# Attention and soft mixture of experts: products on a tile of ones before the first loads, the first turned pairs in another PSUM ring, a new order of the first pair, and its negated row maxima on ScalarE

## The chip, the cores and the metric

The kernel runs on one core of a Trainium2 chip. The time is the device time of one execution in microseconds (us). Beside plain runs there is one profiled execution, whose trace gives each instruction of each engine: TensorE (PE for the products, PEld for the loads of weights), VectorE (DVE), ScalarE (ACT), GpSimd (POOL) and SyncE (SP).

## The reference

The input is `q`, `k` and `v` for 8 batches, 12 heads, 448 positions and 64 features a head, and a soft mixture of experts with 32 slots, 8 experts, a model width of 768 and a hidden width of 1024. In short:

```
scores = scale * q @ k.T                       # per batch and head, 448 x 448
m      = max(scores, -1);  e = exp(scores - m)
x      = (e / (sum(e) + exp(-m) + 1e-9)) @ v   # heads side by side: 3584 x 768
logits = x @ phi                               # 3584 x 32
slot_in  = softmax(logits over the rows).T @ x # 32 x 768
slot_out = relu(slot_in @ w1[e]) @ w2[e]       # four slots for each expert
out      = softmax(logits over the slots) @ slot_out
```

## The kernel before, in words

Two heads make a **pair**; there are 48 pairs (`NPAIR`), six to a batch, and three pairs (`NP`) make a group `g` of loads. The order of all instructions is written out by hand (`manual_schedule`, L59), and each engine takes its own instructions in the order of the program. Loads are issued from POOL's queue (`gdma`, L57), the results at the end from SP's.

The work on pair `n` has these parts:

- `T(n)` (L214) turns q and k with 28 small transposes on PE (L224) into one PSUM bank `ps_t`; ACT copies the bank to SBUF for `n < 6` (L227, a "T copy" below).
- `A(n, i)` (L237), four a pair, multiplies query rows by all keys (L246, L256) into banks `ps_a`, and DVE takes the row maximum of each (L250, L259). For `i < 3` there are two banks and two maxima (one for each head `hl`), for `i = 3` one bank and one maximum; a pair has 7 maxima. `A1(n, i, hl)` (L261) does one head of an `A` alone.
- `W1(g)` (L273) writes the negated maxima on POOL: three instructions into the rows `wm` (the function `neg`, L277), then `ngm`, a rounded copy. `W2(g)` (L293) turns `wm` on PE into a bank `ps_m`, and `W3(g)` (L301) copies that on ACT to `mT` (L303) and takes two small exponentials (L306, L309).
- `Bk(n, i)` (L313) makes the scores with the keys as rows in banks `ps_b`: the product (L332), then a product that subtracts the maxima from `mT` (L335), then ACT's exponential (L338). From half-step 5 on, `AB` (L342) does the same with an `A1` around it (L354, L358, L360, maxima L268, L270).
- `AV(n, i, ...)` (L381) multiplies by v into the one bank `ps_av`; `N1`, `N2` (L399, L408) divide; `PX` (L438) turns the result, and `P(b)` (L458) does the softmax of the slots for a batch.

PSUM has three rings in this part: `psA` with three banks (tag "a": `ps_a`, `ps_t` and the banks of `P`), `psB` with four (tag "b": `ps_b`, `ps_m`, `ps_x`) and `psV` with one. A tile takes the next bank of its ring and waits until the last reader of that bank is done.

The main loop (L635) goes over the pairs `s`, each in two half-steps `hs = 2s + y`. In the half-steps 0 to 4 each does four `A` of later pairs (`As(1)`, four times), two `Bk` of pair `s`, one `T(hs + 3)` and, from half-step 1 on, an `AV`. Ahead of the loop stands a prologue (L610 to L625): `T(0)`, `A` 0 and 1 of pair 0, `T(1)`, `A` 2 and 3, `W1(0)`, the copy `V(0)` of v on POOL, a load of v, `A(1, 0)`, `T(2)`, `W2(0)`, `W3(0)`, `A(1, 1)`, then loads of group 2 and four rewrites of weights (`narrow`, L136). The first half-step starts with `A(1, 2)`. The loads of group 0 (one for each pair), of v and of group 1 are the first instructions of the program (L170 to L177), with `make_identity` between them; DVE's fills (L190 to L201) stand behind.

Of the kernel before, what the change touches and what calls it, by code (L numbers as in the profile page):

```python
# [8 lines left out]
F32 = mybir.dt.float32  # L9
BF16 = mybir.dt.bfloat16  # L10
AX = mybir.AxisListType
AF = mybir.ActivationFunctionType
ALU = mybir.AluOpType
# [11 lines left out]
HG = 6  # L25
NP = 3
W65 = 65
# [4 lines left out]
def kernel(  # L32
# [10 lines left out]
    nc = tc.nc  # L43
    B, H, S, D = q.shape
# [27 lines left out]
    ones = const.tile([128, 2], BF16, name="ones")  # L72
    sel = const.tile([128, HG], BF16, name="sel")
    phi_sb = const.tile([128, KC, NS], BF16, name="phi_sb")
    halfm = const.tile([128, 2], F32, name="halfm")
# [13 lines left out]
    part = lambda nm, o, z: R[:, at_[nm] + o:at_[nm] + o + z]  # L89
# [3 lines left out]
    vp = [part(f"vp{i}", 0, VPN).rearrange("p (h i d) -> p h i d", h=HG, i=4) for i in range(2)]  # L93
    wm = [part(f"wm{i}", 0, 512).rearrange("p (i c) -> p i c", i=4) for i in range(2)]
# [48 lines left out]
    with ExitStack() as at:  # L143
# [3 lines left out]
        psA = pool("psA", 3, space=PSUM)  # L147
        psB = pool("psB", 4, space=PSUM)
# [5 lines left out]
        def load(g, nm, l0=0, l1=NP):  # L154
# [12 lines left out]
                gdma(out=t[64:128], in_=x[:, :, 3:7, :])  # L167
            nat[nm, g] = t

        for pl in range(NP):  # L170
            load(0, "q", pl, pl + 1)
            load(0, "k", pl, pl + 1)
            if pl == 0:
                make_identity(nc, ident)
# [9 lines left out]
        for base in (0, 64):  # L184
# [2 lines left out]
                out=sel[base:base + 64], in_=sel[base:base + 64], fill=1.0,  # L187
                compare_op=ALU.not_equal, base=0,
                pattern=[[-1, HG]], channel_multiplier=1)
        nc.vector.memset(halfm, 0.0)  # L190
        for hl in range(2):
            nc.vector.memset(halfm[64 - 64 * hl:128 - 64 * hl, hl:hl + 1], 1.0)
        for t in wm:
            nc.vector.memset(t, 0.0)
        for t in vp:
            nc.vector.memset(t, 0.0)
            nc.vector.memset(t[:, :, 0:3, D:W65], 1.0)
            nc.vector.memset(t[0:64, 0:HG:2, 3, D:W65], 1.0)
            nc.vector.memset(t[64:128, 1:HG:2, 3, D:W65], 1.0)
        nc.vector.memset(ones, 1.0)  # L200
        nc.vector.memset(ones[64:128, 1:2], 0.0)  # L201
        gdma(out=phi_sb, in_=moe_phi.rearrange("(j p) s -> p j s", p=128))

        mx, ngm, ec, mT, eT, av, us = {}, {}, {}, {}, {}, {}, {}
# [8 lines left out]

        def T(n):  # L214
            g, pl = divmod(n, NP)
            ps = psA.tile([128, 2, S], BF16, tag="a", name="ps_t")
            for a in range(2):
                src = nat["qk"[a], g]
                for tok in range(7):
                    for hl in range(2):  # L220

                        c = kcol(hl, tok) if a else (2 * tok if tok < 4 else 2 * tok - 7) * 64
                        r = slice(64 * hl, 64 * hl + 64)
                        nc.tensor.transpose(ps[r, a, c:c + 64], src[r, pl, tok * D:(tok + 1) * D], ident[r, r])  # L224
            t = qk_t[n % NQK]
            if n < 6 or pl == 0:
                nc.scalar.copy(t, ps)  # L227
            else:
                nc.vector.tensor_copy(t, ps)  # L229
            qkT[n] = t  # L230
# [30 lines left out]
        def A1(n, i, hl):  # L261

            g, pl = mg(n), n % NP
            if pl == mpl(g)[0] and i == 0 and hl == 0:
                mx[g] = psm.tile([128, 21], F32, tag="mx", name="mx")
            t, r = qkT[n], slice(64 * hl, 64 * hl + 64)
            ps = psA.tile([128, 512], F32, tag="a", name="ps_a")
            nc.tensor.matmul(ps[:, 0:S], t[r, 0, i * 128:(i + 1) * 128], t[r, 1, :], start=True, stop=True)  # L268
            c = HG * i + 2 * pl + hl
            nc.vector.reduce_max(mx[g][:, c:c + 1], ps[:, 0:S], axis=AX.X)  # L270


        def W1(g):  # L273
            w, m = wm[g % 2], mx[g]
            l0, l1 = mpl(g)
            nm = psm.tile([128, 21], BF16, tag="ngm", name="ngm")
            neg = lambda o, s: nc.gpsimd.tensor_scalar(o, s, -1.0, None, op0=ALU.mult)  # L277
            cols = lambda t: t[:, 0:3 * HG].rearrange("p (i c) -> p i c", i=3)[:, :, 2 * l0:2 * l1]
            o = w[:, 0:3, :].rearrange("p i (d c) -> p i d c", d=2)[:, :, :, 2 * l0:2 * l1]
            neg(o, cols(m).unsqueeze(2).to_broadcast([128, 3, 2, 2 * (l1 - l0)]))  # L280
            for hl in range(2):
                r = slice(64 - 64 * hl, 128 - 64 * hl)
                o = w[r, 3, :].rearrange("p (d c) -> p d c", d=2)[:, :, 2 * l0 + hl:2 * l1:2]
                neg(o, m[r, 3 * HG + l0:3 * HG + l1].unsqueeze(1).to_broadcast([64, 2, l1 - l0]))
            if l1 - l0 == NP:
                neg(nm, m)
            else:
                nc.gpsimd.memset(nm, 0.0)
                neg(cols(nm), cols(m))
                neg(nm[:, 3 * HG + l0:3 * HG + l1], m[:, 3 * HG + l0:3 * HG + l1])  # L290
            ngm[g] = nm
# [313 lines left out]
        def As(c):  # L605
            for _ in range(min(c, len(runs))):
                A(*runs.pop(0))


        T(0)  # L610
        As(2)
        T(1)
        As(2)
        W1(0)
        V(0)
        load(1, "v")
        As(1)
        T(2)
        W2(0)
        W3(0)  # L620
        As(1)
        for nm in "qk":
            load(2, nm)
        for z in range(4):
# [10 lines left out]
        for s in range(NPAIR):  # L635
# [57 lines left out]
            g = (s + 10) // 3  # L693
# [193 lines left out]
```

## Time and profile before

| what | value |
|---|---|
| median of 3 runs | 310.43 us (310.2 to 311.73) |
| profiled execution | 310.7 us |
| its span, first to last instruction | 308.9 us |
| busy in the span | PE 275.6, DVE 257.2, ACT 249.3, POOL 202.7 us |
| chain of waits that ended last | PE 50%, DVE 30%, ACT 7% |

A line of the timeline has the start, the length, the engine, the source line (L224 is line 224), the operation, what it writes and reads, how many instructions are merged in it, and in brackets how long the engine had idled and what ended that. A line of the page's groups has the busy time, the mean of one instruction in ns and the idle time before.

### The profile page before, as it was taken

What the parts mean: (1) busy time and instruction counts of PE and PEld (TensorE: products, weight loads), DVE (VectorE), ACT (ScalarE), POOL (GpSimd) and SP (SyncE); (2) the same over time, 40 slices, a digit from 0 to 9 for tenths busy, and PEclk for the clock granted to TensorE, in tenths of its full rate; (3) what the DMA queues carried; (4) which work ended last, traced back from release to release, by engine and by line L of the source; (5) the groups of instructions that cost most, each with busy time, mean ns of one, the idle gap of its engine ahead of it and who ended that gap; (6) DMA issues with size and microseconds to landing.
All of it is one profiled execution on the core that took longest, in us unless ns stands there. A gap on an engine that the chain in (4) does not pass through costs nothing.

```text
span 308.9 us, 12205 instructions
## 1 busy us (share of the span) xinstructions
PE 275.6 (89%) x5067; PEld 159.0 (51%) x5068; DVE 257.2 (83%) x607; ACT 249.3 (81%) x549; POOL 202.7 (66%) x403
## 2 busy tenths in 40 slices
PE   2899999999999999999999999999999899994810
PEld 1434456565666656665566566656665556451200
DVE  4778999999999999999999999999999566536930
ACT  2357599999999999999999999999999997236810
POOL 8682769788788878896889788879584863000000
PEclk9999999999999999999999999999999999999555
DMA  6999499999999999999999999999971999937997
GB/s 88 149 128 202 64 205 150 198 182 205 163 196 157 210 169 198 155 203 149 149 164 186 177 186 169 196 177 203 166 110 17 144 126 204 337 128 260 415 439 312
DMA packets 49350, 57.44 MB, mean 186 GB/s; under 512 B 2832, under 2 KB 41488, under 8 KB 48912
## 3 DMA queue, kind: packets, MB, share of 16 engines
q0 software_dynamic: 45536, 42.52, 90.1%
q1 hardware_dynamic: 3760, 14.16, 11.5%
q8 instruction: 39, 0.64, 0.8%
q14 instruction: 15, 0.12, 0.1%
HBM read 88.18 MB, written 14.16 MB: 331 GB/s over the span
## 4 chain that ended last, share of the span: by engine, by line
PE 50%; DVE 30%; ACT 7%; issue 4%; POOL 4%; DMA 1%; DVEq 0%; POOLq 0%
DVE mx L270 15%; PE ps_av L393 11%; PE ps_a L268 6%; PE ps_t L224 6%; PE ps_b L354 5%; PE ps_b L358 4%; DVE mx L250 3%; DVE mx L259 3%; PE ps_b L332 3%; PE ps_a L246 2%; DVE W L801 2%; DVE R L229 2%; PE ps_x L445 2%; ACT R L227 2%; PE ps_so L764 2%
## 5 line engine op out<-in xcount | busy, mean ns | idle before, releaser
L270 DVE TENSOR_REDUCE mx<-ps_a 128x1 f32<-128x448 f32 x248 | 136.6, 613 | 5.3 <-PE ps_a L268 5.1
L360 ACT ACTIVATE R<-ps_b 128x448 bf16<-128x448 f32 x272 | 131.0, 573 | 1.1 <-PE ps_b L358 0.8
L268 PE MATMUL ps_a<-R 64*128 64x448 bf16 x248 | 80.5, 352 | 1.8 <-DVE mx L270 1.8
L354 PE MATMUL ps_b<-R 64*128 64x448 bf16 x272 | 73.9, 353 | 0.9
L358 PE MATMUL ps_b<-mT,sel 64*128 64x448 bf16 x272 | 70.6, 350 | 0.0
L393 PEld LDWEIGHTS <-R 128*128 128x128 bf16 (+1 forms) x1536 | 50.5, 101 | 30.5 <-issue 26.4
L393 PE MATMUL ps_av<-R 128*128 128x65 bf16 (+1 forms) x1536 | 64.9, 196 | 0.1
L419 POOL TENSOR_TENSOR R<-ubuf,rec 128x384 bf16<-128x384 f32 x44 | 36.3, 825 | 37.9 <-DVE rec L415 23.4
L224 PEld LDWEIGHTS <-R 64*64 64x64 bf16 x1344 | 31.1, 113 | 19.2 <-issue 7.8
L338 ACT ACTIVATE R<-ps_b 128x448 bf16<-128x448 f32 x64 | 36.0, 579 | 5.9 <-PE ps_b L335 5.9
L224 PE MATMUL ps_t<-ident,R 64*64 64x64 bf16 x1344 | 32.0, 198 | 5.9 <-DMA R<-in_q_dram 4.3
L451 ACT CAST R<-ps_x 128x512 bf16<-128x512 f32 x47 | 28.1, 598 | 5.7 <-PE ps_x L445 5.7
L259 DVE TENSOR_REDUCE mx<-ps_a 128x1 f32<-128x448 f32 x48 | 29.6, 616 | 0.6 <-PE ps_a L256 0.3
L358 PEld LDWEIGHTS <-sel 64*128 64x128 bf16 x272 | 21.5, 94 | 14.9 <-issue 5.3
L268 PEld LDWEIGHTS <-R 64*128 64x128 bf16 x248 | 23.1, 94 | 9.8
L405 ACT COPY ubuf<-ps_av 128x455 f32<-128x455 f32 x44 | 25.2, 573 | 3.0 <-PE ps_av L393 2.8
L227 ACT COPY R<-ps_t 128x896 bf16<-128x896 bf16 x20 | 18.4, 922 | 11.3 <-PE ps_t L224 11.0
L250 DVE TENSOR_REDUCE mx<-ps_a 128x1 f32<-128x448 f32 x40 | 22.6, 618 | 4.3 <-PE ps_a L246 3.9
L332 PE MATMUL ps_b<-R 64*64 64x448 bf16 (+1 forms) x112 | 22.7, 386 | 0.0
L335 PE MATMUL ps_b<-mT,sel 64*64 64x448 bf16 (+1 forms) x112 | 21.5, 366 | 0.0
L424 POOL TENSOR_TENSOR R<-ubuf,rec 128x128 bf16<-128x128 f32 x44 | 17.5, 398 | 3.7
L354 PEld LDWEIGHTS <-R 64*128 64x128 bf16 x272 | 17.2, 94 | 4.7 <-issue 0.2
(132 smaller groups left out, 454.0 us busy)
## 6 DMA issues: line engine op xcount, KB each, us to landing
W<-in_moe_w_dram POOLq DMA_DIRECT2D x22, 768.0 KB, 9.5
R<-in_v_dram POOLq DMA_DIRECT2D x32, 192.0 KB, 4.6
out_dram<-W SPq DMA_DIRECT2D x2, 2688.0 KB, 10.3
R<-in_q_dram POOLq DMA_DIRECT2D x15, 336.0 KB, 7.4
R<-in_k_dram POOLq DMA_DIRECT2D x15, 336.0 KB, 8.5
wd<-in_moe_w_dram POOLq DMA_DIRECT2D x8, 384.0 KB, 10.0
R<-wd SPq DMA_DIRECT2D x8, 384.0 KB, 8.6
R<-in_moe_w_dram POOLq DMA_DIRECT2D x2, 768.0 KB, 8.3
```

What stands on the lines that cost most here:

```text
L224: nc.tensor.transpose(ps[r, a, c:c + 64], src[r, pl, tok * D:(tok + 1) * D], ident[r, r])
L250: nc.vector.reduce_max(mx[g][:, c:c + 1], pss[hl][:, 0:S], axis=AX.X)
L259: nc.vector.reduce_max(mx[g][:, c:c + 1], ps[:, 0:S], axis=AX.X)
L268: nc.tensor.matmul(ps[:, 0:S], t[r, 0, i * 128:(i + 1) * 128], t[r, 1, :], start=True, stop=True)
L270: nc.vector.reduce_max(mx[g][:, c:c + 1], ps[:, 0:S], axis=AX.X)
L332: nc.tensor.matmul(outs[hl], t[rs[hl], 1, cols], t[rs[hl], 0, :], start=True, stop=False)
L338: nc.scalar.activation(e, p[:, 0:S], AF.Exp, scale=scale)
L354: nc.tensor.matmul(ps[hl][:, 0:S], t[rs[hl], 1, cols], t[rs[hl], 0, :], start=True, stop=False)
L358: nc.tensor.matmul(ps[hl][:, 0:S], sel[rs[hl], h:h + 1].to_broadcast([64, 128]), mT[mg(n)][rs[hl], :], start=False, stop=True)
L360: nc.scalar.activation(e[:, hl, :], ps[hl][:, 0:S], AF.Exp, scale=scale)
L393: nc.tensor.matmul(o, eT[n, i, hl][:, qc], vp[g % 2][:, 2 * pl + hl, i, 0:W65], start=(i == 0 and u == 0 and hl == 0), stop=(i == 3), skip ...
L419: eng.tensor_mul(x[:, 0:3, c:c + 128].rearrange("p i (h d) -> p i h d", h=2), u[:, 0:6, 0:D].rearrange("p (i h) d -> p i h d", h=2), rec[: ...
```

## The change

Six edits, all of them in the first microseconds:

1. A tile of 512 columns, `warm_t`, is filled with ones by DVE ahead of all else. `warm(n, cols)` multiplies it by itself `n` times into a bank of `psV` that nobody reads: seven products of 512 columns before the first transposes, two of 448 behind `T(0)`, one of 448 ahead of `A(0, 3)`.
2. DVE's fills move ahead of the first loads in the program; `ident2`, `identf` and `sel` come behind.
3. `T(n)` for `n < 6` takes its bank from `psB`, not `psA`.
4. The prologue is in another order: `A(0, 1)` is split, with `T(1)` between its heads; `T(2)` stands ahead of `W1(0)`; `A(1, 1)` is split, with `W2(0)` and `W3(0)` between its heads.
5. `W1(0)` writes its three instructions into `wm` on ACT (`rows`); `ngm` stays on POOL, and so do all later `W1`.
6. A helper `As1` does the halves.

```diff
+        warm_t = part("e2", 0, 512)
+        nc.vector.memset(warm_t, 1.0)
+        ps_w = psV.tile([128, 512], F32, tag="v", name="ps_warm")
+
+        def warm(n, cols=512):
+            for _ in range(n):
+                nc.tensor.matmul(ps_w[:, 0:cols], warm_t[:, 0:128], warm_t[:, 0:cols], start=True, stop=True)
...
+        warm(7)
+        for pl in range(NP):
+            load(0, "q", pl, pl + 1)
...
-            ps = psA.tile([128, 2, S], BF16, tag="a", name="ps_t")
+            tp, tg = (psB, "b") if n < 6 else (psA, "a")
+            ps = tp.tile([128, 2, S], BF16, tag=tg, name="ps_t")
...
+            rows = (lambda o, s: nc.scalar.mul(o, s, -1.0)) if g == 0 else \
+                (lambda o, s: nc.gpsimd.tensor_scalar(o, s, -1.0, None, op0=ALU.mult))
...
-            neg(o, cols(m).unsqueeze(2).to_broadcast([128, 3, 2, 2 * (l1 - l0)]))
+            rows(o, cols(m).unsqueeze(2).to_broadcast([128, 3, 2, 2 * (l1 - l0)]))
...
-                neg(o, m[r, 3 * HG + l0:3 * HG + l1].unsqueeze(1).to_broadcast([64, 2, l1 - l0]))
+                rows(o, m[r, 3 * HG + l0:3 * HG + l1].unsqueeze(1).to_broadcast([64, 2, l1 - l0]))
...
+        def As1(hl):
+            A1(*runs[0], hl)
+            if hl:
+                runs.pop(0)
+
         T(0)
-        As(2)
+        warm(2, S)
+        As(1)
+        As1(0)
         T(1)
-        As(2)
+        As1(1)
+        As(1)
+        warm(1, S)
+        As(1)
+        T(2)
         W1(0)
         V(0)
         load(1, "v")
         As(1)
-        T(2)
+        As1(0)
         W2(0)
         W3(0)
-        As(1)
+        As1(1)
```

More of the change, by code (lines that the diff above doesn't have):

```diff
@@ L168, in load @@
             nat[nm, g] = t
+        warm_t = part("e2", 0, 512)
[4 more added lines that the diff above has]
+                nc.tensor.matmul(ps_w[:, 0:cols], warm_t[:, 0:128], warm_t[:, 0:cols], start=True, stop=True)
+        nc.vector.memset(halfm, 0.0)
+        for hl in range(2):
+            nc.vector.memset(halfm[64 - 64 * hl:128 - 64 * hl, hl:hl + 1], 1.0)
+        for t in wm:
+            nc.vector.memset(t, 0.0)
+        for t in vp:
+            nc.vector.memset(t, 0.0)
+            nc.vector.memset(t[:, :, 0:3, D:W65], 1.0)
+            nc.vector.memset(t[0:64, 0:HG:2, 3, D:W65], 1.0)
+            nc.vector.memset(t[64:128, 1:HG:2, 3, D:W65], 1.0)
+        nc.vector.memset(ones, 1.0)
+        nc.vector.memset(ones[64:128, 1:2], 0.0)
+        warm(7)
         for pl in range(NP):
@@ L189 @@
                 pattern=[[-1, HG]], channel_multiplier=1)
[L190 to L201, printed above, removed]
         gdma(out=phi_sb, in_=moe_phi.rearrange("(j p) s -> p j s", p=128))
```

## Prediction

> **What bounds the kernel now.** I read the page first, then the waits, then the timeline of the first 30 us, then the groups of VectorE in that stretch. On the page:
>
> ```profile
> DVE  4778999999999999999999999999999566536930
> ...
> PEclk9999999999999999999999999999999999999555
> DMA  6999499999999999999999999999971999937997
> ...
> PE 50%; DVE 30%; ACT 7%; issue 4%; POOL 4%; DMA 1%; DVEq 0%; POOLq 0%
> ```
>
> From the fourth slice to the thirtieth DVE has nines, and yet the chain that ended last has more of PE than of DVE: the two release each other in turn, a machine in balance, in which a delay at the start is carried to the end. The first three slices (23 us) are thinner (4, 7, 7). The change touches only them. Of the answer on waits one line bears on loads:
>
> ```profile
> PE ps_t L224 <- DMA R<-in_q_dram: 4.3, 1, 4.3
> ```
>
> PE waits for a load once, for the first q; no later wait of PE, DVE or ACT for a load stands in that answer. The early timeline, cut to what the sum needs:
>
> ```profile
> 4.35 1.11 PE L224 MATMUL ps_t<-ident,R 64*64 64x64 bf16 x28 [4.35 <-DMA R<-in_q_dram]
> 5.50 0.91 ACT L227 COPY R<-ps_t 128x896 bf16<-128x896 bf16 x1 [3.47 <-PE ps_t L224]
> 7.06 2.22 DVE L250 TENSOR_REDUCE mx<-ps_a 128x1 f32<-128x448 f32 x4
> 16.08 0.56 PE L332 MATMUL ps_b<-R 64*128 64x448 bf16 x2
> 16.42 0.58 PE L335 MATMUL ps_b<-mT,sel 64*128 64x448 bf16 x2
> 19.47 0.56 PE L246 MATMUL ps_a<-R 64*128 64x448 bf16 x2 [0.32 <-DVE mx L250]
> 22.08 0.96 PE L224 MATMUL ps_t<-ident,R 64*64 64x64 bf16 x28
> 22.97 0.82 PE L393 MATMUL ps_av<-R 128*128 128x65 bf16 x12
> 24.12 2.22 DVE L250 TENSOR_REDUCE mx<-ps_a 128x1 f32<-128x448 f32 x4 [0.71 <-PE ps_a L246]
> 25.76 0.36 PE L332 MATMUL ps_b<-R 64*128 64x448 bf16 x2
> 25.96 0.35 PE L335 MATMUL ps_b<-mT,sel 64*128 64x448 bf16 x2
> 26.93 0.63 PE L224 MATMUL ps_t<-ident,R 64*64 64x64 bf16 x28 [0.18 <-DVE mx L259]
> 28.60 1.69 DVE L250 TENSOR_REDUCE mx<-ps_a 128x1 f32<-128x448 f32 x3 [0.67 <-PE ps_a L246]
> ```
>
> Two things are to be seen. First, **PE runs at half its rate until about 23 us**: L335 starts 0.34 us behind L332 at 16.1, and 0.20 behind it at 25.8; 28 transposes take 0.96 us at 22.08 and 0.63 at 26.93. PEclk has nines from the first slice, so that row doesn't show it; the products' spacing does. Second, DVE's gaps end on a product of `A` (0.71 and 0.67 us, <-PE ps_a). And a transposing `T` at full rate still waits for DVE (0.18 <-DVE mx L259), because `ps_t` takes its turn in the ring of the maxima's banks. How much DVE idles up to the 31st maximum, at 28.60, is in one row of the windows for DVE and in two of the groups:
>
> ```profile
> 7.00:28.58 21.58, 17.00 (x31) 1.00 1.14 155
> ```
> ```profile
> L250 DVE TENSOR_REDUCE mx<-ps_a 128x1 f32<-128x448 f32 x26 | 14.7, 618 | 3.4 <-PE ps_a L246 3.3
> L259 DVE TENSOR_REDUCE mx<-ps_a 128x1 f32<-128x448 f32 x4 | 2.5, 622 | 0.6 <-PE ps_a L256 0.3
> ```
>
> 30 maxima took 17.0 us, 0.567 each back to back, in 21.58: **4.58 us idle**. That is all there is to win without making a maximum shorter.
>
> The Trainium skill, "TensorE: Matmul & The Clock Gate", Part 1, has a rule for the first point: the array starts at half rate, and a free-running window of about 3.4 us with PE busy opens it. The trace agrees in that the last idle time of PE before the turn ends at 19.5 us and the full rate comes some 4 us later.
>
> **The change part by part.** *The seven products ahead of the loads.* The trace has no fill of 512 columns of ones and no such product at half rate. Bounds from these rows:
>
> ```profile
> 1.25 0.71 POOL L162 DMA_DIRECT2D R<-in_q_dram  x1 [0.79 <-POOLq L871]
> 1.95 0.55 POOL L162 DMA_DIRECT2D R<-in_k_dram  x1
> 3.59 0.54 POOL L162 DMA_DIRECT2D R<-in_k_dram  x1
> 3.85 0.55 DVE L194 MEMSET R<- 128x256 uint32 x2
> 4.51 0.72 DVE L196 MEMSET R<- 128x792 uint32 x1
> ```
> ```profile
> R<-in_k_dram POOLq DMA_DIRECT2D x1, 112.0 KB, 2.9
> ```
>
> 256 elements cost 0.27 (0.55 for two), 792 cost 0.72, so 512 about 0.48. POOL's first issue comes at 1.25, behind 0.79 of idle time, so from 0.46 on an engine may start; the ones are there at 0.95 to 1.75. A product of 448 columns follows the one before by 0.34 at half rate, so one of 512 by 0.39 (an estimate), and seven by 2.7. They end at 3.7 to 4.5. `T(0)` starts at 4.35 now; its second half needs the first k, issued at 1.95 and landed 2.9 later, at 4.85, so it ends near 5.4 in any case, and at 5.8 if a late last product and its drain hold it up by 0.3. At full rate the first pair's products come 0.1 to 0.2 earlier (0.20 against 0.34). Bounds at the start: 0.2 gained to 0.3 lost; I take 0, nearest to the 4.35 row. The two products behind `T(0)` (0.7) lie under the T copy (0.91); the one ahead of `A(0, 3)` lies in a wait for a bank.
>
> *DVE's fills* (0.48 + 0.55 + 2 x 0.72 and small ones, about 3 us) lie beside the first loads, and DVE has nothing else until 7.06. They cost nothing unless they hold up POOL: k issued at 3.59, beside the fills, took 0.54, against 0.55 for k at 1.95 with DVE idle. The Trainium skill, "SBUF — State Buffer", section "SBUF: two separate sides", says that some forms of DVE's work lock POOL out, so that it can't write its transfers' descriptors. These two rows disagree for the fills; were it so, the time would be that of the third rival.
>
> *Ring, order, full rate.* A half-step needs seven maxima of DVE, 7 x 0.567 = 4.0 us. PE at full rate: four `A` and four halves of `Bk`, eight pairs of products 0.20 apart, `T` 0.63, and `AV` 0.54 (0.82 x 0.63 / 0.96), about 2.8 us; at half rate 8 x 0.34 + 0.96 + 0.82 = 4.5. So at full rate PE is ahead of DVE, at half rate it is not. And a `T` in psB no longer waits for a maximum, so no gap as that of 0.67 at 28.60 stands behind `T(3)` to `T(5)`. `T(6)` and `T(7)` stay in psA, and half-steps 3 and 4 keep their length.
>
> With DVE dense from 7.06, maximum k starts at 7.06 + 0.567 (k - 1). Who could be late for it? The rows:
>
> ```profile
> 7.21 0.84 POOL L162 DMA_DIRECT2D R<-in_k_dram  x1
> 11.10 0.25 POOL L277 TENSOR_SCALAR R<-mx 128x12 bf16<-128x12 f32 x1 [1.47 <-DVE mx L250]
> 11.82 0.52 POOL L277 TENSOR_SCALAR R<-mx 64x2 bf16<-64x2 f32 x2 [0.47 <-DVE mx L259]
> 12.85 0.66 POOL L374 COPY R<-R 128x576 bf16<-128x576 bf16 x1
> 13.51 0.54 ACT L303 CAST mT<-ps_m 128x448 bf16<-128x448 f32 x1
> 13.93 0.23 ACT L306 ACTIVATE ec<-ngm 128x18 f32<-128x18 bf16 x1
> 14.05 0.21 ACT L309 ACTIVATE ec<-ngm 128x3 f32<-128x3 bf16 x1
> 17.79 2.97 POOL L137 DMA_DIRECT2D wd<-in_moe_w_dram  x4
> 34.10 1.94 ACT L338 ACTIVATE R<-ps_b 128x448 bf16<-128x448 f32 x4 [1.13 <-PE ps_b L335]
> ```
> ```profile
> R<-in_k_dram POOLq DMA_DIRECT2D x1, 336.0 KB, 8.0
> ```
>
> - `W2(0)`: maximum 7 ends at 11.0. `T(2)` stands behind `A(0, 3)`, which gets the bank of maximum 4 at 9.3; with its product (0.2) and its transposes (0.63 to 0.96) and the copy (0.91) ACT is free at 11.1 to 11.4. Then come three small instructions on ACT, which no row shows. L306 takes 0.23, L309 0.21, and they start 0.12 apart; so 0.45 (0.12 + 0.12 + 0.21) to 0.65 (three in a row). `W2(0)`, some tenths, holds PE till then; behind it is `A(1, 1)`'s second head, maximum 11, due at 12.7, just in time. On POOL they take 0.25 + 0.52 from maximum 7 on, to 11.9; on ACT they end at 11.5 to 12.0: from 0.4 gained to 0.1 lost, all of it under the cover of the maxima queued; I take 0.
> - `T(3)` needs k of group 1. It is issued at 7.21 and lands 8.0 later, at 15.2. `T(3)` would be asked for at 14.4 and so waits 0.8, a wait that isn't there now. Behind it on PE is `A(2, 1)`, maximum 17, due at 16.1; it is ready at 15.9. Just covered.
> - `W1(1)` stands on POOL behind `V(0)` and its issues. `V(0)` starts at 12.85 now and the last of them ends at 20.76 (17.79 + 2.97), 7.9 later; it can start behind `ngm` at 11.5, so they end at 19.4. Its rows then end at 20.2 (0.77 more), `W2(1)` holds PE till then, and behind it is maximum 26, due at 21.2. Covered by 0.3 or so.
>
> Three covers of 0.1 to 0.3 are thin, and semaphores cost some hundredths at every handover; I leave DVE 0.6 idle. Sum: 4.58 - 0.6 + 0 = **4.0 us earlier at maximum 31**. From there all engines, POOL's issues too, follow the same order as before, 4.0 earlier. The profiled execution (310.7, 1.8 above its span) would be 306.7; set against the median of the runs, 310.4 - 4.0 = **306.4 us**. Bounds: no idle left and 0.2 at the start and some 0.4 in half-steps 3 and 4 give 305.2.
>
> **Rivals.**
> - *The rate stays at half until about 20 us.* Then half-steps 1 and 2 last 4.5, not 4.0 (1.0 lost); `A(1, 0)` comes behind a `T(2)` slower by 0.33; `W2` and the first `Bk` are slow too (an estimated 0.4). 306.4 + 1.7 = **308.1**. For it: the gap ahead of 19.47 was only 0.32 us, and PE had not turned fast by then. Against: with three products between, the new order keeps PE at work from 1.3 to 6.2. By the same skill page's Part 4 transposes don't count as work for the gate, which would make this rival of it.
> - *The gain is given back behind the early stage.* DMA has nines in most slices; if loads, not engines, set the pace later, everything from the middle on lies where it lay: **310.4**. Against: no engine waits for a load after 4.35.
> - *The fills hold POOL's issues.* The first load leaves behind the last fill, near 3.9, not at 1.25: 2.7 lost, **309.1**. Against: the 0.54 and 0.55 of the two issues above.
> - *Slower: psB.* Six T copies (0.91 each) now hold banks of the exponentials' ring. If ACT is behind by a half-step, each holds up the next `Bk`, and PE with it: 6 x 0.91 = 5.5 lost, **311.9**. It decides when ACT's work in a half-step passes DVE's 4.0. Four exponentials (1.94), a T copy (0.91) and `W3` (0.54 + 0.12 + 0.21) are 3.7 at most. So it speaks against, thinly.
>
> **How the numbers follow.** Forecast 306.4: 0.62. Half rate, 308.1: 0.16. Given back, 310.4: 0.11. Fills, 309.1: 0.04. psB, 311.9: 0.07. Half a per cent, 1.55 us, is about what a measurement here can tell from no change; faster takes the first two (0.78), same the next two (0.15), slower the last (0.07). The range goes from 305.2, the bound above, to 308.6, the first rival with a late start (0.3) and 0.2 of stalls, and leaves out the three last cases (0.22).
>
> **What would show it.** Right: L335 0.20 behind L332 in the first `Bk`; 28 transposes in about 0.63 by `T(2)` or `T(3)`; the 31st maximum near 24.6; 310.7 less that shift at the end. Wrong: 0.34 spacings past 12 us (first rival); a wait for in_k at `T(3)` with DVE idle behind it; a DVE gap before maximum 11 released by `W2`; the first q issued later than 1.3; `Bk` waiting for a T copy; the 31st maximum 4 earlier and the end not.

## The result and the profile after

The kernel after takes 308.99 us in the median of 22 runs (306.58 to 311.53), the kernel before beside it 311.22 (22 runs): a ratio of 0.9921 [0.99, 0.9942], 2.45 us or 0.8% faster. The ratio leaves out the two runs of the kernel after that are over 1.5% longer than its fastest; the medians of all runs lie 2.23 us apart. That ratio on the 310.43 us of the prediction is 307.98. Forecast were 4.0 us, a ratio of 0.987, so the direction came and some 60% of the size; the median itself lies 0.4 above the forecast range, and 0.8 us of its distance from the forecast is that the kernel before came out at 311.22 here, not at 310.43. The profiled execution took 307.67 us with a span of 305.9, where before it was 310.7 and 308.9: 3.0 less.

The same rows of the page as before (DVE, DMA, the chain that ended last), now of the kernel after:

```profile
DVE  5989999999999999989999999999999476536930
...
DMA  6999999999999999998999999999962899927997
...
PE 47%; DVE 27%; POOL 8%; ACT 7%; issue 5%; DMA 2%; DVEq 0%; POOLq 0%
```

DVE is dense from the second slice on (two eights among the nines) instead of the fourth. In the chain POOL went from 4% to 8% and DMA from 1% to 2%. The early timeline of the kernel after (start, length, engine, line, operation, what the engine had waited for), cut to the rows that are read here, tells where both stand:

```profile
4.56 0.95 PE L234 MATMUL ps_t<-ident,R 64*64 64x64 bf16 x28
7.12 1.16 DVE L260 TENSOR_REDUCE mx<-ps_a 128x1 f32<-128x448 f32 x2 [1.83 <-PE ps_a L256]
7.21 0.63 PE L234 MATMUL ps_t<-ident,R 64*64 64x64 bf16 x28
11.15 0.67 ACT L285 ACTIVATE R<-mx 128x12 bf16<-128x12 f32 x3
12.31 0.67 POOL L386 COPY R<-R 128x576 bf16<-128x576 bf16 x1 [1.07 <-DMA R<-in_v_dram]
15.26 0.41 PE L234 MATMUL ps_t<-ident,R 64*64 64x64 bf16 x14 [0.41 <-DMA R<-in_k_dram]
15.99 2.22 DVE L260 TENSOR_REDUCE mx<-ps_a 128x1 f32<-128x448 f32 x4 [0.29 <-PE ps_a L256]
17.26 2.98 POOL L137 DMA_DIRECT2D wd<-in_moe_w_dram  x4
20.32 0.90 POOL L286 TENSOR_SCALAR R<-mx 128x24 bf16<-128x24 f32 x3
20.66 0.34 PE L309 MATMUL ps_m<-ident,R 128*128 128x128 bf16 x3 [0.72 <-POOL R L286]
21.81 1.16 DVE L260 TENSOR_REDUCE mx<-ps_a 128x1 f32<-128x448 f32 x2 [0.69 <-PE ps_a L256]
23.38 0.63 PE L234 MATMUL ps_t<-ident,R 64*64 64x64 bf16 x28
23.93 0.79 PE L405 MATMUL ps_av<-R 128*128 128x65 bf16 x20
24.65 0.55 PE L256 MATMUL ps_a<-R 64*128 64x448 bf16 x3
25.05 2.22 DVE L260 TENSOR_REDUCE mx<-ps_a 128x1 f32<-128x448 f32 x4 [0.41 <-PE ps_a L256]
```

Read it from the end. The 31st maximum starts at 25.05, not at 28.60: **3.55 us earlier** (forecast 4.0). DVE's largest late gap (0.69) ends on a product that stood behind `W2(1)` (L309), which waited 0.72 for POOL's rows (L286); these rows follow four issues of weights (17.26 to 20.24), the issues follow the loads of group 2, those follow `V(0)` (L386), and `V(0)` waits 1.07 us for **v to land**, at 12.2. The wait in front of `T(3)` for k (0.41) stands there too and costs DVE 0.29. The gap of 0.41 right before maximum 31 is of another kind: PE waits for nothing there, but a `T` and the 20 products with v of an `AV` stand in one piece ahead of the next `A` (23.38 to 24.65). That gap, 0.41 or 0.42, stands there in every profile with `T` in psB, whichever cover holds. The chain that ended last runs the same way; its pieces (start, length, what) in order of time:

```profile
5.83 6.35 DMA R<-in_v_dram
12.31 0.68 POOL R L386
...
17.27 1.53 POOL wd L137 x3
19.16 1.08 POOL wd L137
```

And the windows of DVE over the stretch that held 4.58 us of idle time before (columns: stretch, length, busy, instructions, clock, DMA share, GB/s):

```profile
7.04:25.03 17.99, 16.39 (x30) 1.00 1.19 159
```

1.60 us are left idle, not 0.6; the 30 maxima themselves took 16.39 rather than 17.0, since more of them run back to back. The idle time beyond the forecast (1.0), less what the maxima gained (0.61), and a first maximum 0.06 later make the 0.45 that is missing here. Of the 1.60, 0.69 stand behind `W2(1)`, 0.41 behind the `AV`, 0.29 behind `T(3)`, and 0.16 at 19.97.

From maximum 31 on the two profiles lie 3.55 us apart up to 125 us. Between 129 and 136 us the distance falls to 3.03, and there it stays to the end. No wait for a buffer or an engine is new there. PE itself stops, inside a burst of small products whose operands had long been ready (the second row's idle time is put down to nothing but the issue):

```profile
135.04 0.18 PE L551 MATMUL ps_s<-cd,ones 128*128 128x32 bf16 x1
135.65 0.23 PE L551 MATMUL ps_s<-cd,ones 128*128 128x32 bf16 x3 [0.43 <-issue]
```

### The profile page after: what moved, and what is told of

Same layout as the page of the kernel before. It is cut to its first block, busy times and chain, and to the rows that moved or that the text cites. A ratio compares the mean times of both kernels' runs of the same rounds, so it can differ in the third digit from the quotient of the medians.

```text
span 305.9 us, 12225 instructions
## 1 busy us (share of the span) xinstructions
PE 274.5 (90%) x5077; PEld 157.9 (52%) x5078; DVE 257.0 (84%) x608; ACT 249.7 (82%) x552; POOL 202.8 (66%) x400
## 4 chain that ended last, share of the span: by engine, by line
PE 47%; DVE 27%; POOL 8%; ACT 7%; issue 5%; DMA 2%; DVEq 0%; POOLq 0%
DVE mx L280 14%; PE ps_av L405 11%; PE ps_a L278 6%; PE ps_b L366 5%; PE ps_t L234 4%; PE ps_b L370 4%; PE ps_b L344 3%; DVE mx L269 2%; DMA R<-in_v_dram 2%; DVE W L824 2%; PE ps_x L457 2%; PE ps_so L787 2%; PE ps_h L771 2%; DVE mx L260 2%; DVE R L239 2%
## 5 line engine op out<-in xcount | busy, mean ns | idle before, releaser
L278 PE MATMUL ps_a<-R 64*128 64x448 bf16 x252 | 82.1, 352 | 2.0 <-DVE mx L280 1.8
L234 PEld LDWEIGHTS <-R 64*64 64x64 bf16 x1344 | 29.7, 110 | 14.6 <-issue 6.1
L234 PE MATMUL ps_t<-ident,R 64*64 64x64 bf16 x1344 | 31.0, 194 | 1.7 <-DMA R<-in_k_dram 0.4
L278 PEld LDWEIGHTS <-R 64*128 64x128 bf16 x252 | 23.6, 94 | 10.0
L344 PE MATMUL ps_b<-R 64*64 64x448 bf16 (+1 forms) x112 | 21.6, 371 | 0.0
L347 PE MATMUL ps_b<-mT,sel 64*64 64x448 bf16 (+1 forms) x112 | 20.4, 349 | 0.1
L436 POOL TENSOR_TENSOR R<-ubuf,rec 128x128 bf16<-128x128 f32 x44 | 17.6, 400 | 3.7
## 6 DMA issues: line engine op xcount, KB each, us to landing
out_dram<-W SPq DMA_DIRECT2D x2, 2688.0 KB, 10.3
```

The lines of the kernel that those rows point to most:

```text
L344: nc.tensor.matmul(outs[hl], t[rs[hl], 1, cols], t[rs[hl], 0, :], start=True, stop=False)
```

## The experiments

All ratios are to the kernel before on the same chip. "Maximum 31" and "end" are how much earlier than in the first profile of the kernel before (28.60 and 308.9 us) they come in the run's own profile.

| kernel | median us (runs) | before beside it | ratio [95%] | maximum 31 | end |
|---|---|---|---|---|---|
| no_products | 307.96 (6) | 310.77 | 0.9921 [0.9897, 0.9946] | 2.04 | 1.39 |
| products_only | 309.67 (12) | 310.77 | 0.9965 [0.9938, 0.9992] | 1.91 | 1.94 |
| narrow_late | 308.27 (7) | 310.77 | 0.993 [0.9905, 0.9956] | 3.94 | 3.80 |
| before_again | 311.49 (11) | 310.77 | 1.0025 [0.9991, 1.0059] | 1.41 | 1.29 |
| hold | 309.63 (12) | 310.66 | 0.997 [0.9948, 0.9992] | 3.45 | 0.16 |
| hold_late | 309.83 (12) | 310.66 | 0.9985 [0.9963, 1.0007] | 3.04 | -1.14 |
| hold_ring | 311.08 (12) | 310.66 | 1.0021 [0.9997, 1.0044] | 2.37 | -0.53 |
| after_again | 307.23 (6) | 310.66 | 0.9906 [0.9878, 0.9934] | 3.74 | 2.99 |
| hold_128 | 309.44 (12) | 311.12 | 0.9972 [0.9943, 1.0002] | 1.57 | 0.38 |
| shift38 | 309.84 (12) | 311.12 | 0.9959 [0.9927, 0.999] | 3.57 | -0.95 |
| ring_only | 309.44 (12) | 311.12 | 0.9962 [0.9937, 0.9987] | 2.21 | 1.83 |
| rows_pool | 308.23 (9) | 311.12 | 0.9913 [0.9881, 0.9945] | 3.76 | 2.49 |
| hold_lite | 308.82 (12) | 311.01 | 0.9928 [0.9898, 0.9958] | 3.82 | 2.31 |
| hold_aligned | 308.12 (6) | 311.01 | 0.9906 [0.9876, 0.9937] | 2.86 | 2.21 |
| after_third | 307.97 (7) | 311.01 | 0.9902 [0.9867, 0.9937] | 2.64 | 1.90 |

### Which part brings it: no_products, products_only, ring_only, rows_pool

**no_products** is the kernel after without the products on ones:

```diff
-        warm(7)
...
-        warm(2, S)
...
-        warm(1, S)
```

> The changed kernel without its ten products on ones; ring, order, fills and ScalarE's rows stay. Theory 1 (the early full rate carries the gain): the array turns fast at 20 us or later, the 31st maximum comes near 26.5 instead of 25.05, and the time is 1.5 to 2 us above the changed kernel's, about 1 below the kernel before. Theory 2 (ring and order carry it; a denser PE opens the gate by itself): full rate from some 10 to 14 us, the 31st maximum within 0.5 us of 25.05 and the time within 0.6 us of the changed kernel's.

The time is that of the kernel after (both 0.9921), though its profile shows the half rate up to 21.8 us; `T(1)` and `T(4)`, for example, take 0.96 each:

```profile
7.30 0.96 PE L233 MATMUL ps_t<-ident,R 64*64 64x64 bf16 x28
...
20.37 0.96 PE L233 MATMUL ps_t<-ident,R 64*64 64x64 bf16 x28
```

So in the profile the products bring 1.5 us early (3.55 against 2.04), and in the medians nothing that can be measured (each ratio is known to some 0.8 us).

**products_only** does that part alone: the fills and the ten products, with `T` in psA, the old order and the first rows on POOL.

> The kernel before with the fills moved ahead and the ten products, but its own ring, its own order and POOL's rows. Theory 1: full rate from about 7 us, the 31st maximum 2 us or more earlier than 28.60 and the time 1.5 to 2 us below the kernel before. Theory 2: the transposes still wait for maxima, so the 31st maximum is at most 1.5 us earlier and the time 0.5 to 1 us below.

It gains 0.35%. Its windows tell what becomes of the early rate (columns: stretch, length, busy time of PE, PEld, DVE, ACT, POOL, then the granted clock, DMA share, GB/s):

```profile
8.00:12.00 4.00, 3.66 (x66) 2.08 (x66) 3.91 (x8) 1.02 (x2) 2.51 (x11) 0.75 1.25 169
12.00:16.00 4.00, 3.81 (x20) 1.04 (x18) 2.84 (x5) 2.42 (x6) 3.78 (x8) 0.50 0.97 114
```

The rate opened at 6.6 us, fell back to half at 10.0 and came again at 16.8. The clock of 0.75 and 0.50 in these rows shows it. (Ahead of the first change on record that column stands at 1.00, also where the products' lengths show half rate; so it tells a rate that was lost, not one that has not come yet.)

**ring_only** goes the other way from no_products: the order of the prologue is the old one again, and the ring and ACT's rows stay (against no_products):

```diff
-        As(1)
-        As1(0)
+        As(2)
         T(1)
-        As1(1)
-        As(1)
-        As(1)
-        T(2)
+        As(2)
         W1(0)
         V(0)
         load(1, "v")
         As(1)
-        As1(0)
+        T(2)
         W2(0)
         W3(0)
-        As1(1)
+        As(1)
```

> The kernel before with the fills moved, the six T in psB and the first negated rows on ACT, in the old order and without products: against no_products only the order is undone. Theory (ring and order both carry the gain): maximum 31 some 1.2 to 1.8 us before that of the first profile of the kernel before, the median 308.9 to 309.7 against 310.8 (no_products: 308.0). Rival, the ring is all of it and the new order is worth nothing: median 307.8 to 308.3, maximum 31 gains 2.0. Other rival, the order is all of it: median 310.3 or more.

The median fits the first theory (309.44), maximum 31 doesn't (2.21 gained, 1.2 to 1.8 expected): in this execution the rate opened at 17.9 us, in that of no_products at 21.8, and that hides the order in these two profiles. By the medians the ring is worth 1.2 us (0.9962) and the order 1.3 more (0.9921); the intervals of the two ratios still touch.

**rows_pool** puts the first three negated rows back on POOL (`if g == 0` made false).

> The kernel after with the first three negated rows back on POOL, all else as in after. My prediction gave ACT's rows 0 (between 0.4 gained and 0.1 lost, under the cover of queued maxima): median within 0.4 of after's (307.2 to 309), maximum 31 at 24.8 to 25.4. Rival, the rows on POOL hold up V(0), the loads behind it and W1(1) by 0.8: V(0) waits for v's landing at 12.2 anyway, so that can show only if the rows end behind 12.2; then maximum 31 would be at 25.5 to 25.9 and the median 0.4 to 0.8 above after's.

As expected, nothing: 308.23, maximum 31 at 24.85. `V(0)` still waits 0.44 us for v there; POOL had the time. What is late in this execution is k: `T(3)` waits 1.07 us for it, and DVE idles 0.95 behind.

### The third cover: narrow_late

```diff
-        for z in range(4):
-            narrow(z)
...
                 if hs == 1:
                     W1(1)
+                    for z in range(4):
+                        narrow(z)
```

> The changed kernel with the four rewrites of weights issued behind the second W1 instead of ahead of it. If the cover that failed is POOL's queue (its v copy waits until 12.3 for the load of v, so the second W1 starts at 20.32 and its turn on PE holds up maximum 26 by 0.69 us), the second W1 starts near 18.8, that gap goes, the 31st maximum comes at about 24.4 instead of 25.05, and the time falls by 0.5 to 0.7 us. Rival: another wait (the exponentials, or v for the first AV) takes its place and maximum 31 stays within 0.2 us of 25.05.

POOL's rows come 1.5 us earlier than in the kernel after, and the gap of 0.69 in front of the products behind `W2(1)` is 0.16; the timeline of narrow_late:

```profile
18.79 0.28 POOL L286 TENSOR_SCALAR R<-mx 128x24 bf16<-128x24 f32 x1 [1.92 <-DVE mx L260]
20.34 0.34 PE L309 MATMUL ps_m<-ident,R 128*128 128x128 bf16 x3
20.45 2.22 DVE L260 TENSOR_REDUCE mx<-ps_a 128x1 f32<-128x448 f32 x4 [0.16 <-PE ps_a L256]
```

Now the rows wait for maxima, not for POOL. Maximum 31 gains 3.94, the forecast's 4.0, although the array fell back to half rate from 12.5 to 15.9 us in this execution. That POOL's queue makes the gap is shown: with the four issues out of the way the gap goes. What it is worth is not: maximum 1 starts 0.20 earlier here than in the kernel after (6.92 and 7.12), and the same edit on a kernel without that gap (hold_late, below) brings nothing. The median (308.27) doesn't tell it from the kernel after.

### The kernels themselves again: before_again, after_again, after_third

> The kernel before, unchanged, for the granted clock of each of its runs. If the end of the full rate alone spreads the times, the kernel before shows the same range of clocks (0.947 to 0.963) and a slope of 0.3 to 0.5 us for each us of half rate at the end, as the changed kernel does; the gain at equal clocks is then the 3 us of the profiles. If the start differs between runs, times at equal clocks differ by over 1 us.

The median differs from that beside it by nothing measurable. Its profiled execution, though, has maximum 31 at 27.2 us, 1.41 before the first profile's, because the full rate came at 17.6 us and not at 23.6. The profile on which the sum was made was one draw.

> The changed kernel, unchanged, beside the held ones on the same chip. Theory: about half of its runs show a clock below 0.955, and these are 1 to 2.5 us slower than the others; the median is 1 to 2 us above the held kernel's. Rival: its clock does not go with its time.

> The kernel after, unchanged, beside the two others: median 307.2 to 309.2, with a clock of 0.944 to 0.963 from run to run, the runs below 0.954 some 1 to 2 us slower than the rest.

Both repeat the result (0.9906, 0.9902). In both the rate falls back: the windows of after_again, with a granted clock of 0.88 and 0.69,

```profile
8.00:12.00 4.00, 3.32 (x42) 1.32 (x41) 3.99 (x8) 2.16 (x6) 2.20 (x9) 0.88 1.25 167
12.00:16.00 4.00, 3.24 (x33) 1.05 (x32) 3.44 (x6) 2.40 (x7) 3.88 (x8) 0.69 1.13 132
```

and in after_third from 17.5 to 21.0 us. In after_third, though, something else comes first. The timeline of after_third:

```profile
16.03 0.41 PE L234 MATMUL ps_t<-ident,R 64*64 64x64 bf16 x14 [1.18 <-DMA R<-in_k_dram]
16.76 2.22 DVE L260 TENSOR_REDUCE mx<-ps_a 128x1 f32<-128x448 f32 x4 [1.06 <-PE ps_a L256]
```

`T(3)` waits 1.18 us for k, and DVE idles 1.06 behind it (0.29 in the first profile of the kernel after). That is most of why its maximum 31 gains 2.64 only, and the rate falls at the end of that thin stretch. In after_again the wait is 0.76 and the gap 0.65. In these two and in rows_pool the gap of 0.69 behind `W2(1)` is not there. So which cover fails differs from execution to execution, and the one for k fails more often than that for POOL's rows.

The mean clock of a run tells a part of this without a profile. All runs of the kernel before lie at 0.958 to 0.964. One window of 3.41 us at half rate takes some 0.006 off (half of 3.41, in 306 us). No profile without a lost window lies under 0.957 (hold_late, whose half rate at the end is longest), but after_third has 0.957 with one. So a run below 0.956 has lost a window somewhere; one above may have. Of the runs of the kernel after that the three ratios are made of, 17 are at 0.956 or above, with a median of 307.67 us, and 16 below, down to 0.942, with 308.97.

### Is it the rate? hold, hold_late, hold_ring, hold_lite

**hold** adds products where PE is thin, so that the rate is held: eight of 448 columns in the prologue and half-step 0, and a first product of `Bk` done twice for pairs 0 to 2. **hold_late** is hold with the late `narrow`, **hold_ring** is hold with `T` in psA.

```diff
+            if n < 3 and not c:
+                for hl in range(2):
+                    nc.tensor.matmul(outs[hl], t[rs[hl], 1, cols], t[rs[hl], 0, :], start=True, stop=True)
...
         T(1)
+        warm(1, S)
         As1(1)
+        warm(1, S)
...
+        warm(1, S)
         As1(0)
+        warm(1, S)
         W2(0)
```

> The changed kernel with more products that nobody reads: four of 448 columns in the prologue, four in half-step 0, and each first score product of Bk done twice for pairs 0 to 2. Theory: the full rate is taken back in many executions because PE, fast, waits for DVE and streams columns for only about half of a window of 3.41 us; held busier, it stays. Then the granted clock is 0.955 or more in all runs but a few (half rate only at the end), the median falls to 306.5 to 307.5, with a spread of 2 us or less, and the 31st maximum stays near 25. Rival: the spread of the changed kernel comes from elsewhere; then clocks as low as 0.947 remain and the median stays within 0.5 us of the changed kernel's, or rises by the added products.

> The held kernel with the four rewrites issued behind the second W1. At a held full rate the POOL wait is what is left: the 31st maximum comes at 24.3 to 24.6, and the time is 0.4 to 0.7 us below the held kernel's. Rival: another wait takes its place, less than 0.3 us.

> The held kernel with the first turned pairs back in the maxima's ring. If the ring carries part of the gain at full rate, each of T(1) to T(5) again waits for a maximum, DVE idles some 0.4 to 0.7 us behind each of three or four of them, and the time is 1 to 2 us above the held kernel's. Rival: the order alone does it, and the time is within 0.4 us.

The rate held in all three (clocks of hold's runs 0.956 to 0.961), and at maximum 31 hold gained 3.45, but at the end 0.16. This theory fell: more rate, less gain; the kernel after, forecast 1 to 2 us above hold, came 2.4 below it (after_again). hold_late missed its forecast too: its maximum 31 comes at 25.57, not at 24.3 to 24.6, and its median is no better than hold's. Maximum 1 starts 0.42 later in it, and from there to maximum 31 both take 18.50 us; in hold there is no gap behind `W2(1)` to take away. hold_ring against hold, with the same number of PE instructions, is the price of the ring: 1.08 us at maximum 31, 1.45 in the median. hold's timeline at the place of its first loss, at 70 us, within one run of 28 transposes:

```profile
68.76 0.60 PE L234 MATMUL ps_t<-ident,R 64*64 64x64 bf16 x27
69.99 0.19 PE L234 MATMUL ps_t<-ident,R 64*64 64x64 bf16 x1 [0.63 <-issue]
```

27 are done; the 28th, of the same tile, starts 0.82 us behind the 27th, where its neighbours are 0.02 apart. Counted from the start of the program, the stops of this sort, in all kernels, stand at products whose numbers differ by multiples of 128 (a product is two instructions, a weight load and a multiplication): 2400 in the kernel after, 2272 in shift38, 1120 in hold, each of which leaves 96 when divided by 128. The page's table of queues has a row for what a program of 10155 PE instructions loads (here the kernel after):

```profile
q8 instruction: 39, 0.64, 0.8%
```

39 transfers of 16 KB, 256 instructions each. After a stop the first product of a block starts 1.25 to 1.6 us behind the end of the block's transfer; PE stops where it is there sooner, which is the case where the block before was used up quickly, by small products, or the transfer came late. The kernel before has such stops as well (0.27 us at 133.3 and 0.37 at 139.5). A change in the early stage that adds PE instructions moves every later block boundary: hold's 28 products moved them into `T` at 70 us and elsewhere. This is the theory of the blocks; its rival is that hold's products themselves cost the time.

Blocks cost hold time at its end as well, where PE doesn't stop. Its program needs a fortieth block, and that one is transferred at 288.5 us, among the transfers of the results; the page of hold:

```profile
q8 instruction: 40, 0.66, 0.8%
...
out_dram<-W SPq DMA_DIRECT2D x2, 2688.0 KB, 11.9
```

The same transfers of results take 10.3 us in the kernel after, whose last block is there at 274 us. In hold, hold_late, hold_ring, hold_lite and shift38 the last block comes at 286 to 291 us, and from the last result that an engine writes to the end of the span it takes 13.7 to 14.5 us; in the twelve other profiles it is there by 277.3 us, and it takes 12.5 to 12.9. Of the 3.3 us that hold loses behind maximum 31, 1.7 are gone at its last maximum (240 us), and 1.6 go here.

**hold_lite** came later: hold without the doubled products, so with eight products more than the kernel after.

> The kernel after with eight products of 448 columns added in the prologue and the first half-step, so that the array streams over half of each window up to about 17 us; the doubled products of hold are left out. Theory (rate lost again in part of the runs, and stalls by position): the granted clock of the runs stays at 0.956 or more, where after has 0.944 to 0.963; maximum 31 gains 3.3 to 3.9 against the first profile of the kernel before; the stalls near 129 and 136 us stay at about 0.4 to 0.9 together, those of hold near 70, 214 and 226 us are not there; median 307.0 to 308.2, at least 0.5 below that of after beside it. Rival, the added products cost what the rate brings: median as after's, 308 to 309, or above. Other rival, the early rate is of no use at the end: as no_products, ratio 0.990 to 0.994.

The clock held (0.958 to 0.961), maximum 31 gained 3.82, and the median was 308.82, not below the 307.97 of the kernel after beside it. The profile tells why that decides little: no stop is over 0.35 us, also not near 129 and 136 us, where two were expected, and at the last maximum (238 us) hold_lite is still 4.0 ahead of the first profile of the kernel before. The fortieth block then costs it 1.6 at the end. So the added products were tried together with a late block, and what the held rate is worth stays open. The rate isn't all that parts the runs: those of hold_lite, all at one clock, spread from 306.6 to beyond 310.

### Is it the blocks? hold_128, shift38, hold_aligned

**shift38** does the seven products of 512 columns as 45 of 80, nothing else. The work is the same, the count is 38 higher.

```diff
+        def small(n, cols):
+            for _ in range(n):
+                nc.tensor.matmul(ps_w[0:64, 0:cols], warm_t[:, 0:64], warm_t[:, 0:cols], start=True, stop=True)
...
-        warm(7)
+        small(45, 80)
```

> The kernel after with its seven first products of 512 columns cut into 45 of 80 columns: the same work for PE before the first load is there, 38 products more. Theory of the instruction blocks: the early stage stays as in after (maximum 31 at 24.8 to 25.4); the stalls at 129.5 (0.32) and 135.7 us (0.61) are gone; new ones stand 38 products ahead of the old places, near 127 us in the products with v, of 0.7 to 1.3 us, and near 160 us, 0.2 to 0.7; the end 0.2 to 1.2 us later than after's, the median 308.3 to 309.2. Rival, the stalls belong to those stretches of the program (a semaphore, a transfer) and not to the count of instructions: they stay at the T of 129.5 and at the slots' product of 135.7, and the time is after's, 307.2 to 309.

The early stage is as in the kernel after (3.57), the stalls at the old places are gone, and PE stops in the products with v near 127 us, as forecast from the count alone. shift38's timeline there:

```profile
127.05 0.32 PE L409 MATMUL ps_av<-R 128*64 128x65 bf16 x7
129.19 0.19 PE L409 MATMUL ps_av<-R 128*64 128x65 bf16 x1 [1.82 <-issue]
```

2.02 us between two products of one run of eight; the forecast was 0.7 to 1.3. The pause also cost the array its rate from 130.1 to 133.5 us. The second stop was forecast near 160 us; it came at 168.9 (0.66), and two smaller ones followed. The end lies 0.95 *behind* the first profile of before, 1.1 of it through the late last block; the median is 1.6 above that of rows_pool beside it, and above the forecast 308.3 to 309.2. The rival (stalls that belong to their place in the program) is out.

**hold_128** cuts the early products of hold into so many that PE has 128 more than the kernel after: all boundaries fall again where they fell.

> Hold with PE's work of the early stage kept but cut into 100 products more (the first seven of 512 columns become 89 of 64 columns, three later ones of 448 become seven of 64 each), so that PE has 128 products, 256 instructions, more than the kernel after. Theory of the instruction blocks: in the traces so far PE stalls late only at one place in each 256 of its instructions, and hold loses its early gain because its 28 added products move these places into bursts of short products. With 128 added, every place behind the early stage falls where it falls in the kernel after: hold's stalls near 70.0, 213.6 and 226.3 us are gone, those near 129 and 136 us stay as in after (0.3 and 0.6), and the end comes 2.7 to 3.1 us before that of the first profile of the kernel before (hold: 0.2); median 307 to 308.2 against about 310.7. Rival, hold's added products themselves cost the time (PE or the banks are short later, or the array's rate): the end stays at 0 to 0.8 us before, median 309.3 to 310.2, as hold. Early maximum 31 at 24.9 to 25.6 in both.

Its 89 products of 64 columns took 4.95 us where seven of 512 took 3.17, so `T(0)` came 1.8 us late and the early gain is 1.57; I had priced them too low. By its median and its end alone (309.44, 0.38) it fits the rival's forecast; what speaks for the blocks here is where PE stops. Behind that, the stalls of hold at 70, 214 and 226 us are gone, and those at 131.4 (0.31) and 137.6 (0.61) are the kernel after's 129.5 (0.32) and 135.7 (0.61). **hold_aligned** reaches the same count with the small products spread:

```diff
-        warm(7)
+        small(41, 88)
...
-        warm(1, S)
+        small(7, 64)
```

(the last pair of lines at each of its seven places, and `small(14, 64)` for the two `warm(2, S)`)

> Hold with 100 products more in the places of its products on ones (seven of 64 columns for each of 448, 41 of 88 for the first seven), 128 more than the kernel after. Theory of the instruction blocks: maximum 31 gains 3.0 to 3.5 as in hold, the stalls stand near 129 and 136 us and perhaps 175 as in after and rows_pool, and the end gains 1.8 to 3.0 (hold: 0.2), median 307.2 to 308.7. Rival, the doubled products of the first three pairs cost the time by themselves: end 0 to 1, median 309 to 310.

It ends 2.21 us earlier than before, against hold's 0.16, and its ratio is 0.9906 against 0.997. It contains all the doubled products of hold; so these cost nothing measurable, and the blocks, by stops and by the late last one, cost what hold lost. (hold_128 and hold_aligned load 40 blocks too, but the last is there by 277 us.) The last proof needs three kernels that have the same count by 128 (rows_pool, hold_128, hold_aligned). All three stop at the sixth product of one and the same run of twelve, rows_pool:

```profile
174.76 0.33 PE L405 MATMUL ps_av<-R 128*128 128x65 bf16 x5
175.79 0.37 PE L405 MATMUL ps_av<-R 128*128 128x65 bf16 x7 [0.70 <-issue]
```

hold_128:

```profile
176.90 0.33 PE L412 MATMUL ps_av<-R 128*128 128x65 bf16 x5
177.87 0.37 PE L412 MATMUL ps_av<-R 128*128 128x65 bf16 x7 [0.64 <-issue]
```

hold_aligned:

```profile
175.32 0.33 PE L412 MATMUL ps_av<-R 128*128 128x65 bf16 x5
176.07 0.37 PE L412 MATMUL ps_av<-R 128*128 128x65 bf16 x7 [0.42 <-issue]
```

The kernel after has its boundary at that product too, and in its profile didn't stop there: the block's transfer had ended 2.4 us before, not 1.5. So kernels with the same boundaries lose 0 to 0.9 us at one of them from execution to execution, and the three profiles of the kernel after stop for 0.61, 0.89 and 1.17 us near 136 us. That this is also the spread of the unprofiled runs is likely, and not shown.

No version here is faster than the kernel after beyond the intervals; no_products, with fewer instructions, is as fast.

## Why the prediction was right and wrong

- **What bounds it, and that idle time of DVE at the start is carried on:** right. 2.98 of the 4.58 us of idle time went, and the distance of 3.55 stood unchanged for 100 us.
- **Seven products, fills:** right to 0.2 us. The products follow each other by 0.43, not 0.39, and end at 4.64 (forecast 3.7 to 4.5); `T(0)` starts at 4.56 instead of 4.35, the first maximum at 7.12 instead of 7.06; POOL's first issues are where they were. The rival of the fills is out.
- **Ring:** right, and the surest part: 1.1 us early, 1.2 to 1.45 in the medians. The rival of psB, slower, is out: no `Bk` waited for a T copy.
- **ACT's rows 0:** right (rows_pool).
- **"Three covers of 0.1 to 0.3 are thin", 0.6 us of idle time left:** wrong, and the first step that failed; 1.60 were left. Of the three covers, `W2(0)` held, `T(3)` missed by 0.3, and the third failed by 0.7. The sum let `V(0)` "start behind `ngm` at 11.5"; it starts at 12.31, with v. v is issued at 5.17 and 5.83 behind all loads of group 0, and its landing is in no term of the sum, because no engine waited for it before: the timeline there has POOL in `V(0)` at 12.85, late enough not to show it. `T(3)` was priced with k at 15.2; k came at 15.3 in this profile, but at 15.7 to 16.0 in rows_pool, after_again and after_third, and there this cover failed by 0.65 to 1.06 and the third held. A cover has to be checked against everything that it waits for, also what has slack now, and against how much a landing varies.
- **"So no gap as that of 0.67 at 28.60 stands behind `T(3)` to `T(5)`":** wrong by 0.41, and a term that the sum put at nothing. That gap had two parts. `T`'s wait for a maximum is gone; the `AV` behind it stays. The sum took 0.54 for every `AV`, which is that of 12 products; the one behind `T(5)`, ahead of maximum 31, has 20 and takes 0.79, as it did before.
- **"Full rate" from 7 us on:** right at its start (`T(1)` takes 0.63 at 7.21), wrong in that it stays. At full rate PE waits for DVE, or for k, and streams too little to keep the rate: two of the three profiles of the kernel after lose it for a window of 3.41 us before 21 us, and half of its runs, if not more, show a lost window in their clock. The first rival (half rate until about 20 us) is not what happened; the rate opens early and goes for a window at a time. Besides, the half rate up to 23 us that was to be cured was that of one execution: in before_again it ended at 17.6.
- **"From there all engines follow the same order as before, 4.0 earlier":** the step that failed last. The order is the same, but at two boundaries of instruction blocks PE lost 0.52 us more than in the profile before. The ten added products move these boundaries, which shift38 shows to be enough; but no_products, with as many instructions as the kernel before, lost 0.65 us there too (2.04 to 1.39), so when the blocks arrive decides as well.

Of the 1.55 us that are missing in the ratio, 0.45 are gone at maximum 31 and 0.52 at the blocks, both read from the profile. The other 0.6 lie between profile and median; the runs at a lower clock (half of them, 1.3 us slower) would give as much, an estimate. But clock and blocks vary together: hold_lite held the clock with a late last block, and hold_aligned held it without one and was no faster than the kernel after, with a maximum 31 that came 0.7 later than in the first profile of the kernel after. How this rest divides between the rate, k's landing and the blocks stays open.

## What to carry to other kernels

Price a step that is to start earlier against every input it has, the loads that nobody waits for today included. Products that only keep the array's rate up are worth what that rate is worth where PE bounds: here they brought 1.1 us by themselves (products_only) and nothing measurable beside the ring and the order (no_products). In a long unrolled program count PE's instructions: added ones shift the block boundaries of all that follows, and a 0.5% change can be that alone, the end of the program included.

## What the runs showed of the hardware

**Instruction blocks.** PE's program comes in blocks of 256 instructions. There are stops of 0.3 to 2.0 us at a boundary, most of them when small products (32 to 65 columns) have used up a block quickly. With a block transferred among the results, their largest transfers took 11.9 us instead of 10.3 (hold). The Trainium skill, "Runtime: NRT & Kernel Launch", section "Instruction fetch mechanics", has the 16 KiB blocks of 256 instructions, and calls the cost of crossing one mostly hidden. The trace agrees on the size (39 transfers, 0.64 MB) and not on the hiding: 2.02 us in shift38.

**The rate falls back after one thin window.** Within an execution the changes of the granted clock lie on a grid of 3.41 us. The Trainium skill, "TensorE: Matmul & The Clock Gate", Part 1, gives that window, and the half rate as the state after an idle one. Here PE need not be idle. The share of a window in which products stream can be estimated from their columns and rates in these traces (512 columns 0.43 us apart at half rate, 448 columns 0.19 at full). It is 0.32 to 0.50 in the four early windows at whose end the rate fell (products_only, narrow_late, after_again, after_third), and 0.80 to 0.96 in those that opened it. It draws no sharp line: windows with 0.45 to 0.50 kept the rate (after_again, rows_pool, shift38), and one with 0.80 did not open it (no_products). Part 4 of that page says that a transpose doesn't count as PE-busy in the same way. Here transposes seem to count: without them the windows that opened the rate have 0.58 to 0.87, and the one that did not has 0.80.
